# Talking-heads attention and two MLPs: engines a step apart, whole-array scores, values in runs, other operand offsets

## The chip, the cores and the metric

The kernel runs on one core of a Trainium2 chip. The metric is the device time of one execution in microseconds, the median of a few runs. The engines are TensorE (PE; PEld is its weight load), VectorE (DVE), ScalarE (ACT), GpSimd (POOL) and the queue of SyncE (SP), which issues all DMAs.

## What is computed

Four batches of 12 heads, 448 positions, head size 64; then two MLPs on the 1792 x 768 result.

```python
scores = scale * np.matmul(q, k.transpose(0, 1, 3, 2))
scores = np.einsum('bhij,hg->bgij', scores, w_pre)
scores = scores - np.max(scores, axis=-1, keepdims=True)
attn = np.exp(scores)
attn = attn / (np.sum(attn, axis=-1, keepdims=True) + 1e-09)
attn = np.einsum('bhij,hg->bgij', attn, w_post)
x = np.matmul(attn, v)            # then x as rows of 768
h = x @ w_in                      # MLP 1: where(h > 0, h, exp(min(h, 0)) - 1) @ w_out
h = x @ w_in                      # MLP 2: square(max(h, 0)) @ w_out
```

## The kernel before

Precise products are made of fp32r parts: a number is split into a high part (a rounding copy, `hi`) and the rest (`lo`), and three matmuls, hi with hi, hi with lo and lo with hi, add up in one PSUM bank. mix_post and values use plain fp32, for which the trace has two records a matmul.

**Attention** goes through 16 chunks, four a batch, of 120 or 110 queries (`CHUNKS`, L20). `scores` (L156) makes one pair of heads: the keys and queries of the even head lie on partitions 0 to 63, those of the odd one on 64 to 127, so that two 64-row matmuls work side by side, three passes a pair; ScalarE copies both results to `sc`. For each group of ten queries there is a step `t`, 180 in all: `gather` (L174) fetches the group's rows of all heads by DMA, `split` (L180) makes its parts (ScalarE `gh`, GpSimd `gl`), `mix_pre` (L188) mixes the heads in three matmuls, takes the maximum (VectorE) and the exponential with its sum (ScalarE), `weigh` (L201) folds the sum into the weights of the second mix (VectorE), and `mix_post` (L210) mixes again, four matmuls, which VectorE copies to `at`. `values` (L226) multiplies two heads of a chunk by v, in two halves of the array's columns side by side, 8 matmuls (16 records) a call, six calls a chunk; after three calls VectorE copies the result to `xs`.

The order is written out by hand (L319 ff.): step t gathers for t + 8, mixes for t + 2, weighs for t + 1, then makes the scores that are due (one pair in every second step), splits for t + 5, does the other extras (a values call in every second step, loads, splits of keys and queries) and then mix_post of t. Each engine and the DMA queue of SP take their instructions in that order. PSUM has eight banks: three for scores ("qk"), two for "mix", two for "post", one for "pv" (`BANKS`, L45).

**MLPs** (`Mlps.run`, L540): two halves of 896 rows; in each half four layers, of 576, 576, 576 and 672 matmuls. The first three move 448 columns of activations over 128 x 128 of weights; the last one moves 384 columns of weights. `Weights` loads, converts and splits the weights a few units ahead. The first byte of the moving and of the stationary operand in a line of 256 bytes is set by `MOVING` and `STATIONARY` (L25, L26), by half and layer: in the first half 128 and 224 everywhere; in the second half moving 192, 64, 128, 192 and stationary 224, 224, 96, 224. `plan` (L482) puts the first weights and the first MLP's inputs into the last steps of attention.

Of the kernel before, what the change touches and what calls it, by code (L numbers as in the profile page):

```python
# [24 lines left out]
MOVING = (128, 128, 128, 128), (192, 64, 128, 192)  # L25
STATIONARY = (224, 224, 224, 224), (224, 224, 96, 224)  # L26
# [5 lines left out]
def talking_heads_two_mlps(ctx: ExitStack, tc: tile.TileContext, qr, kr, vr, w_pre, w_post, diagonal,  # L32
# [8 lines left out]
    attention(tc, psum, qr, kr, vr, w_pre, w_post, diagonal, xd, mlps)  # L41
# [3 lines left out]
BANKS = {"qk": 3, "mix": 2, "post": 2, "pv": 1}  # L45
# [6 lines left out]
def attention(tc, psum, qr, kr, vr, w_pre, w_post, diagonal, xd, mlps):  # L52
    nc = tc.nc
    with ExitStack() as ctx:
# [6 lines left out]
        AHEAD, SPLIT, PRE = 8, 5, 2  # L61
# [7 lines left out]
        rows = work.tile([120, NR], F32, name="rows")  # L69

# [36 lines left out]
        kh, kl, kraw, qs, qraw = {}, {}, {}, {}, {}  # L107

        def load_k(b, j, raw=None, pairs=((0, 2),)):

            raw = early.tile([128, 2, S], F32, name="kraw", bufs=2) if raw is None else raw
            src = kr[b, :, 4 * j * S : (4 * j + 4) * S].rearrange("d (p a j) -> d a p j", p=2, a=2)
            for x, y in pairs:
                for a in range(2):
                    nc.sync.dma_start(out=raw[64 * a : 64 * a + 64, x:y], in_=src[:, a, x:y])
            kraw[b, j] = raw

        def split_k(b, p, hi_copy=nc.scalar.copy, engine=nc.gpsimd):

            j, a = divmod(p, 2)  # L120
            if a == 0:
                kh[b, j] = early.tile([128, 2, S], F32R, name="kh", bufs=4)
                kl[b, j] = early.tile([128, 2, S], F32R, name="kl", bufs=4)
            raw, hi, lo = (x[b, j][:, a, :] for x in (kraw, kh, kl))
            hi_copy(hi, raw)
            engine.tensor_tensor(lo, raw, hi.bitcast(F32), ALU.subtract)

        def load_q(n, i, raw=None):

            b, c = chunks[n]  # L130
            raw = early.tile([128, 3, CH + 1], F32, name="qraw", bufs=2)[:, :, :CH] if raw is None else raw
            at = (c * H + 6 * i) * CH
            src = qr[b, :, at : at + 6 * CH].rearrange("d (p a i) -> d a p i", p=3, a=2)
# [4 lines left out]
        def split_q(n, i, engine=nc.gpsimd):  # L138
            if i == 0:
                qs[n] = [early.tile([128, H // 2, CH], F32R, name=f"qs{a}", tag=f"qs{a}", bufs=2) for a in "hl"]  # L140
            raw, (hi, lo) = qraw.pop((n, i)), (x[:, 3 * i : 3 * i + 3, :] for x in qs[n])
            nc.vector.tensor_copy(hi, raw)
            engine.tensor_tensor(lo, raw, hi.bitcast(F32), ALU.subtract)

# [9 lines left out]
        sc = {}  # L154

        def scores(n, p, tags=("qk", "qk"), copies=(nc.scalar.copy, nc.scalar.copy)):  # L156

            b, c = chunks[n]
            if p == 0:
                sc[n] = score[(n + 1) % 2].tile([CH, H, S], F32, name="sc", bufs=1)  # L160
            out = [bank(psum, tag)[:CH, :S] for tag in tags]
            h, l = 0, 1
            for k, (x, y) in enumerate(((h, h), (h, l), (l, h))):
                for a in range(2):
                    o = slice(64 * a, 64 * a + 64)
                    nc.tensor.matmul(out[a], qs[n][x][o, p, :], (kh, kl)[y][b, p // 2][o, p % 2, :],  # L166
                                     start=(k == 0), stop=(k == 2))
            for a in range(2):
                copies[a](sc[n][:, 2 * p + a, :], out[a])  # L169


        graw, parts, ex, wg, at, xs, pv = {}, {}, {}, {}, {}, {}, {}
# [7 lines left out]
        def split(t, engine=nc.gpsimd):  # L180
            x = graw.pop(t)
            hi = work.tile([120, S], F32R, name="gh", bufs=SPLIT - PRE + 1)
            lo = work.tile([120, S], F32R, name="gl", bufs=SPLIT - PRE + 1)
# [4 lines left out]
        def mix_pre(t):  # L188
# [5 lines left out]
            nmax = work.tile([120, 1], F32, name="nmax", bufs=PRE + 2)  # L194
            nc.vector.tensor_reduce(nmax, p, AX.X, ALU.max, negate=True)  # L195
            e = work.tile([120, S], F32, name="ex", bufs=PRE + 1)
            tot = work.tile([120, 1], F32, name="tot", bufs=PRE + 2)
            nc.scalar.activation(e, p, AF.Exp, bias=nmax, scale=1.0, accum_out=tot)  # L198
            ex[t] = e, tot

        def weigh(t):  # L201
            e, tot = ex[t]
            nc.vector.tensor_scalar_add(tot, tot, 1e-9)  # L203
            rec = work.tile([120, 1], F32, name="rec", bufs=4)
            nc.vector.reciprocal(rec, tot)
            w = work.tile([120, 120], F32, name="wg", bufs=3)
            nc.vector.tensor_scalar_mul(w.rearrange("p (a k) -> p a k", a=3), post[:, :, :40], rec)  # L207
            wg[t] = w

        def mix_post(t):  # L210
# [3 lines left out]
            e, _ = ex.pop(t)  # L214
# [4 lines left out]
            o, p = at[n][:, :, :, g * NR : (g + 1) * NR], p.rearrange("p c (g r) -> p c g r", r=NR)  # L219
            if t < last:  # L220
                nc.vector.tensor_copy(o, p)  # L221
            else:
                nc.vector.tensor_copy(o[:, :3], p[:, :3])
                nc.scalar.copy(o[:, 3], p[:, 3])

        def values(n, i):  # L226
# [3 lines left out]
            if c == 0 and i == 0:  # L230
                xs[b] = work.tile([128, KC, S], F32, name="xs", bufs=1)
# [90 lines left out]
        for t in range(T):  # L322
# [4 lines left out]
            if t + 1 < T:  # L327
                weigh(t + 1)
# [342 lines left out]
```

## Time and profile before

| | |
|---|---|
| median of 3 runs | 1405.91 us (1405.33 to 1406.09) |
| the profiled execution | 1404.66 us |
| its span | 1402.9 us |
| mean granted TensorE clock | 0.996 |
| TensorE busy | 1388.5 us (99%), 8908 matmul records |
| its weight loads | 1241.3 us (88%) |
| VectorE, ScalarE, GpSimd busy | 876.6, 678.2, 260.7 us |
| DMA | 174.41 MB, queue q1 38.4% of 16 engines |
| first mix_post, first MLP matmul | at 25.73 us, at 465.36 us |

The span is the time from the first to the last instruction of the profiled execution; the rest of its time lies around it. Busy times of engines overlap. A busy TensorE need not be at its peak: matmuls are pipelined, and the time from one start to the next says what one costs.

### The profile page before, as it was taken

What the parts mean: (1) busy time and instruction counts of PE and PEld (TensorE: products, weight loads), DVE (VectorE), ACT (ScalarE), POOL (GpSimd) and SP (SyncE); (2) the same over time, 40 slices, a digit from 0 to 9 for tenths busy, and PEclk for the clock granted to TensorE, in tenths of its full rate; (3) what the DMA queues carried; (4) which work ended last, traced back from release to release, by engine and by line L of the source; (5) the groups of instructions that cost most, each with busy time, mean ns of one, the idle gap of its engine ahead of it and who ended that gap; (6) DMA issues with size and microseconds to landing.
All of it is one profiled execution on the core that took longest, in us unless ns stands there. A gap on an engine that the chain in (4) does not pass through costs nothing.

```text
span 1402.9 us, 24375 instructions
## 1 busy us (share of the span) xinstructions
PE 1388.5 (99%) x8908; PEld 1241.3 (88%) x8908; DVE 876.6 (62%) x2020; ACT 678.2 (48%) x1507; POOL 260.7 (19%) x241
## 2 busy tenths in 40 slices
PE   8999999999999999999999999999999999999998
PEld 5777778787777899999999999999999999999998
DVE  6877777777788699866699997634441123443121
ACT  5776676676667576533255543235551113333111
POOL 2575565475557000000000000000000000000000
PEclk8999999999999999999999999999999999999999
DMA  4633542543625455554455576531221111112131
GB/s 144 182 112 109 182 131 103 176 140 107 193 99 168 164 175 169 192 173 159 136 162 169 167 239 207 166 113 52 57 75 46 60 45 46 51 51 63 40 107 40
DMA packets 104907, 174.41 MB, mean 124 GB/s; under 512 B 22771, under 2 KB 82259, under 8 KB 104787
## 3 DMA queue, kind: packets, MB, share of 16 engines
q1 hardware_dynamic: 104787, 172.85, 38.4%
q8 instruction: 70, 1.15, 0.3%
q14 instruction: 50, 0.41, 0.1%
HBM read 97.93 MB, written 36.18 MB: 96 GB/s over the span
## 4 chain that ended last, share of the span: by engine, by line
PE 97%; DVE 1%; DMA 0%; SPq 0%; issue 0%; ACT 0%; POOL 0%; DVEq 0%; POOLq 0%
PE ps_post L218 12%; PE ps_qk L537 8%; PE ps_qk L538 8%; PE ps_qk L536 8%; PE ps_pv L237 6%; PE ps_mix L536 6%; PE ps_post L537 6%; PE ps_mix L537 6%; PE ps_mix L538 6%; PE ps_post L538 6%; PE ps_post L536 6%; PE ps_qk L166 5%; PE ps_pv L537 3%; PE ps_pv L538 3%; PE ps_pv L536 3%; PE ps_mix L193 3%
## 5 line engine op out<-in xcount | busy, mean ns | idle before, releaser
L423 ACT CAST wh<-wf 128x384 fp32r<-128x384 f32 (+1 forms) x240 | 126.7, 532 | 271.5 <-DVE wf L409 112.2
L424 DVE TENSOR_TENSOR wl<-wf,wh 128x384 fp32r<-128x384 f32 (+1 forms) x240 | 140.4, 588 | 159.2 <-ACT wh L423 154.5
L185 POOL TENSOR_TENSOR gl<-graw,gh 120x448 fp32r<-120x448 f32 x178 | 203.0, 1141 | 194.7 <-ACT gh L184 167.9
L218 PE MATMUL ps_post<-wg,ex 120*112 120x120 f32 x1440 | 189.4, 275 | 3.0 <-DVE wg L207 2.9
L218 PEld LDWEIGHTS ps_post<-wg,ex 120*112 120x112 f32 x1440 | 165.3, 178 | 29.7 <-issue 10.7
L198 ACT ACTIVATE ex<-ps_mix,nmax 120x448 f32<-120x448 f32 x180 | 114.3, 635 | 129.0 <-DVE tot L203 123.9
L221 DVE COPY at<-ps_post 112x480 f32<-112x480 f32 x161 | 105.4, 655 | 68.6 <-PE ps_post L218 67.5
L195 DVE TENSOR_REDUCE nmax<-ps_mix 120x1 f32<-120x448 f32 x180 | 111.8, 621 | 2.8 <-PE ps_mix L193 2.2
L537 PE MATMUL ps_qk<-xl,wh 128*128 128x448 f32 x288 | 105.3, 365 | 0.0
L538 PE MATMUL ps_qk<-xh,wl 128*128 128x448 f32 x288 | 105.2, 365 | 0.0
L536 PE MATMUL ps_qk<-xh,wh 128*128 128x448 f32 x288 | 104.9, 364 | 0.0
L184 ACT CAST gh<-graw 120x448 fp32r<-120x448 f32 x180 | 102.4, 571 | 0.4 <-DMA graw<-sc 0.4
L237 PEld LDWEIGHTS ps_pv<-at,v 112*64 112x64 f32 x1536 | 74.1, 136 | 29.4 <-issue 20.6
L237 PE MATMUL ps_pv<-at,v 112*64 112x110 f32 (+2 forms) x1536 | 93.9, 265 | 1.3 <-DVE xs L242 0.7
L169 ACT COPY sc<-ps_qk 120x448 f32<-120x448 f32 x176 | 84.6, 534 | 7.1 <-PE ps_qk L166 6.4
L558 DVE TENSOR_TENSOR tmp<-tmp 128x448 f32<-128x448 f32 x64 | 39.9, 624 | 73.7 <-ACT tmp L557 73.7
L191 PE MATMUL ps_mix<-gh,pre_l 120*120 120x448 f32 x180 | 80.0, 444 | 3.0 <-ACT gh L184 3.0
L385 ACT ACTIVATE wf<-wd 128x384 f32<-128x384 f32 (+1 forms) x120 | 69.3, 577 | 16.0 <-DMA wd<-w1i 10.8
L562 DVE TENSOR_TENSOR hl<-tmp,hh 128x448 fp32r<-128x448 f32 x128 | 74.2, 619 | 0.4
L409 DVE SCALAR_TENSOR_TENSOR wf<-wd,wf 128x384 int32<-128x384 int32 (+1 forms) x120 | 70.3, 586 | 4.1
L407 DVE SCALAR_TENSOR_TENSOR wf<-wd,wf 128x384 int32<-128x384 int32 (+1 forms) x120 | 70.2, 585 | 4.1
L537 PE MATMUL ps_mix<-xl,wh 128*128 128x448 f32 x192 | 70.2, 365 | 0.0
(166 smaller groups left out, 3298.4 us busy)
## 6 DMA issues: line engine op xcount, KB each, us to landing
graw<-sc SPq DMA_DIRECT2D x180, 210.0 KB
wd<-w1i SPq DMA_DIRECT2D x32, 384.0 KB
wd<-w1o SPq DMA_DIRECT2D x24, 512.0 KB
wd<-w2i SPq DMA_DIRECT2D x32, 384.0 KB
wd<-w2o SPq DMA_DIRECT2D x32, 384.0 KB
w1if<-wf SPq DMA_DIRECT2D x32, 192.0 KB
w1of<-wf SPq DMA_DIRECT2D x24, 256.0 KB
w2if<-wf SPq DMA_DIRECT2D x32, 192.0 KB
```

What stands on the lines that cost most here:

```text
L184: nc.scalar.copy(hi, x)
L185: engine.tensor_tensor(lo, x, hi.bitcast(F32), ALU.subtract)
L195: nc.vector.tensor_reduce(nmax, p, AX.X, ALU.max, negate=True)
L198: nc.scalar.activation(e, p, AF.Exp, bias=nmax, scale=1.0, accum_out=tot)
L218: nc.tensor.matmul(p[:, c, :], e[:, c * NJ : (c + 1) * NJ], w, start=True, stop=True)
L221: nc.vector.tensor_copy(o, p)
L237: nc.tensor.matmul(pv[n][o : o + 64, i % 3, :w], vt[b, i // 3][:, jc, g % 6 * D : (g % 6 + 1) * D], at[n][:, jc, g, :w], start=(jc == 0), ...
L423: nc.scalar.copy(hi, f)
L424: nc.vector.tensor_tensor(lo, f, hi.bitcast(F32), ALU.subtract)
L536: mm(p, wh, xh, start=first, stop=False)
L537: mm(p, wh, xl, start=False, stop=False)
L538: mm(p, wl, xh, start=False, stop=last)
```

## The change

- **Order in a step.** Groups are gathered nine steps ahead, split six, mixed four; the maximum and exponential (`maxima`) become a function of their own, three ahead. Copies out of PSUM stand a step behind the matmuls that filled the bank: `keep_scores`, `keep_weighed` and `keep_x` empty lists that `scores`, `mix_post` and `values` filled in the step before. `weigh` does two steps at once. The banks are 2 "qk", 3 "mix", 2 "post", 1 "pv".
- **Scores on the whole array** (all chunks but the first four): each query and key is loaded twice, so that partition 2d + a holds entry d. `split_k` subtracts `odd` times the rounded key, with `odd` 0 or 1 by partition, which leaves the high part on even partitions and the low part on odd ones in one tile `kp`. A head then is two matmuls, the queries' hi and lo against `kp`, and is put into a step alone (or two, where twelve heads don't fit nine or ten steps). `odd` is made by two memsets, a DMA to DRAM and one back. The casts of these keys and queries are ScalarE's, the subtractions GpSimd's.
- **Values.** The six calls of a chunk stand in two runs of three, in steps 1 and 2 of the next chunk, behind mix_post. Each run's result goes to DRAM on its own, four steps later, instead of once a batch.
- **MLPs.** `MOVING, STATIONARY = 128, 224` for both halves. The first two units' `part` is split over two steps (`part_hi`, `part_lo`), and the bank order ends in "mix" instead of "qk".

The order on TensorE in an early chunk of attention, before (L191 to L193 are mix_pre, L166 scores, L237 values, L218 mix_post):

```order
L191 MATMUL ps_mix<-gh,pre_l 120x448
L192 MATMUL ps_mix<-gh,pre_h 120x448
L193 MATMUL ps_mix<-gl,pre_h 120x448
L166 MATMUL ps_qk<-kh,qsh 120x448 x2
L166 MATMUL ps_qk<-kl,qsh 120x448 x2
L166 MATMUL ps_qk<-kh,qsl 120x448 x2
L237 MATMUL ps_pv<-at,v 64x110 x8
L218 MATMUL ps_post<-wg,ex 112x120 x4
L191 MATMUL ps_mix<-gh,pre_l 120x448
L192 MATMUL ps_mix<-gh,pre_h 120x448
L193 MATMUL ps_mix<-gl,pre_h 120x448
L218 MATMUL ps_post<-wg,ex 112x120 x4
```

And now (L252 to L254 are mix_pre, L228 and L229 one head's scores, L288 mix_post, L314 values):

```order
L252 MATMUL ps_mix<-gh,pre_l 120x448
L253 MATMUL ps_mix<-gh,pre_h 120x448
L254 MATMUL ps_mix<-gl,pre_h 120x448
L228 MATMUL ps_qk<-kp,qp 120x448
L229 MATMUL ps_qk<-kp,qp 120x448
L288 MATMUL ps_post<-wg,ex 112x120 x4
L252 MATMUL ps_mix<-gh,pre_l 120x448
L253 MATMUL ps_mix<-gh,pre_h 120x448
L254 MATMUL ps_mix<-gl,pre_h 120x448
L288 MATMUL ps_post<-wg,ex 112x120 x4
L314 MATMUL ps_pv<-at,v 64x110 x24
```

Steps with a pair of scores and a values call have become steps with one head, and steps with three values calls in a row.

SP's queue at the start, before (L73, L74 load the mixing weights, L135 the queries of chunk 1, L177 is the gather):

```order
L73 DMA both<-w_pre 120x1x12
L73 DMA both<-w_post 120x1x12
L74 DMA rows<-diagonal 120x10
L135 DMA q_room<-qr 64x3x120 x4
L177 DMA graw<-sc 120x1x448 x9
```

And now (L78, L79 are the two DMAs of `odd`):

```order
L83 DMA both<-w_pre 120x1x12
L83 DMA both<-w_post 120x1x12
L84 DMA rows<-diagonal 120x10
L78 DMA turns_d<-turns 1x128
L79 DMA odd<-turns_d 128x1
L146 DMA q_room<-qr 64x3x120 x4
L238 DMA graw<-sc 120x1x448 x10
```

The queries of chunk 1 stand behind a DMA that waits for another one's landing.

VectorE's queue near the end of attention, around the first subtraction of a weight's parts, before (L223 copies mix_post's result, L195 is the maximum, L203 to L207 `weigh`, L424 the subtraction):

```order
L207 TENSOR_SCALAR wg<-post,rec 120x120
L424 TENSOR_TENSOR wl<-wf_5914,wh 128x384
L223 COPY at<-ps_post 112x36x10
L195 TENSOR_REDUCE nmax<-ps_mix 120x1
L203 TENSOR_SCALAR tot<-tot 120x1
```

And now (L296, L260, L272 to L277 and L532 in the same roles):

```order
L277 TENSOR_SCALAR wg<-post,rec 120x120 x2
L532 TENSOR_TENSOR wl<-wf_5792,wh 128x384
L260 TENSOR_REDUCE nmax<-ps_mix 120x1
L296 COPY at<-ps_post 112x36x10 x2
L272 TENSOR_SCALAR tot<-tot 120x2
```

The subtraction still stands ahead of a maximum, one step behind the cast it reads.

The diff, cut to its core:

```diff
-MOVING = (128, 128, 128, 128), (192, 64, 128, 192)
-STATIONARY = (224, 224, 224, 224), (224, 224, 96, 224)
+MOVING, STATIONARY = 128, 224
-BANKS = {"qk": 3, "mix": 2, "post": 2, "pv": 1}
+BANKS = {"qk": 2, "mix": 3, "post": 2, "pv": 1}
-        AHEAD, SPLIT, PRE = 8, 5, 2
+        AHEAD, SPLIT, MIX, MAX, QN, LATE = 9, 6, 4, 3, 3, 4
+        WIDE = len(CHUNKS)
+        def load_odd():
+            for a in range(2):
+                nc.gpsimd.memset(turns[:, :, a : a + 1], float(a))
+            nc.sync.dma_start(out=turns_d, in_=turns.rearrange("o d a -> o (d a)"))
+            nc.sync.dma_start(out=odd, in_=turns_d.rearrange("o p -> p o"))
+        def twice(out, src):
+            nc.sync.dma_start(out=out, in_=src.unsqueeze(1).broadcast_to([D, 2, src.shape[1]]))
+        def split_k(b, h):
...
+            hi = early.tile([128, S], F32R, name="khi", bufs=1)
+            nc.scalar.activation(hi, raw, AF.Copy, scale=odd)
+            nc.gpsimd.tensor_tensor(k, raw, hi.bitcast(F32), ALU.subtract)
+        def scores(n, h):
...
+            hi, lo = (x[:, h % QN, :] for x in qp[n, h // QN])
+            k = kp[b, h // 2][:, h % 2, :]
+            nc.tensor.matmul(out, hi, k, start=True, stop=False)
+            nc.tensor.matmul(out, lo, k, start=False, stop=True)
+            taken.append((sc[n][:, h, :], out))
+            when = [start + h * steps // H for h in range(H)]
+            for h in range(H):
+                put(when[h], scores, n, h)
+            for i in range(H // QN):
+                put(when[QN * i] - 6, load_q, n, i)
+                put(when[QN * i] - 3, split_q, n, i)
+        for b in range(1, B):
+            for h in range(H):
+                t = first[WIDE * b - 1] - AHEAD + 4 - (H - 1 - h) * 12 // 5
+                put(max(0, t - 4), load_k, b, h)
+                put(t, split_k, b, h)
-                put(first[n + 1] + (2 + i if n == N - 1 else min(2 * i + 1, 10 if n == N - 2 else 11)), values, n, i)
+                put(first[n + 1] + (2 if n == N - 1 else 1) + i // 3, values, n, i)
-                put(first[n] + 9, load_v, b, 1)
+                put(first[n] + 4, load_v, b, 1)
+        for t in range(T + 3):
+            beside = extra.pop(t, ())
+            if t + AHEAD < T:
+                gather(t + AHEAD)
+            keep_scores()
+            if t + SPLIT < T:
+                split(t + SPLIT)
+            if t + MAX < T:
+                maxima(t + MAX)
+            if t + MIX < T:
+                mix_pre(t + MIX)
+            for f, a in beside:
+                if f in (scores, first_scores):
+                    f(*a)
+            store_x(t)
+            keep_weighed()
+            keep_x(t)
+            if t < T:
+                mix_post(t)
+            for f, a in beside:
+                if f is values:
+                    f(*a)
+            weigh(t + 1)
...
```

## Rows read from the trace of the kernel before

**Rows 1.** Page, part 4, the chain that ended last by engine.

```profile
PE 97%; DVE 1%; DMA 0%; SPq 0%; issue 0%; ACT 0%; POOL 0%; DVEq 0%; POOLq 0%
```

**Rows 2.** Timeline of TensorE, attention: start us, us, engine line op, tiles, count.

```profile
301.24 0.44 PE L191 MATMUL ps_mix<-gh,pre_l 120*120 120x448 f32 x1
...
302.81 0.97 PE L237 MATMUL ps_pv<-at,v 112*64 112x110 f32 x16
...
304.55 0.44 PE L191 MATMUL ps_mix<-gh,pre_l 120*120 120x448 f32 x1
...
306.95 0.44 PE L191 MATMUL ps_mix<-gh,pre_l 120*120 120x448 f32 x1
...
309.48 0.45 PE L191 MATMUL ps_mix<-gh,pre_l 120*120 120x448 f32 x1
309.76 0.36 PE L192 MATMUL ps_mix<-gh,pre_h 120*120 120x448 f32 x1
309.96 0.37 PE L193 MATMUL ps_mix<-gl,pre_h 120*120 120x448 f32 x1
...
310.91 0.44 PE L191 MATMUL ps_mix<-gh,pre_l 120*120 120x448 f32 x1
```

**Rows 3.** Timeline of TensorE, end of attention (in brackets: idle before, and releaser).

```profile
454.37 1.05 PE L218 MATMUL ps_post<-wg,ex 120*112 120x120 f32 x8 [2.43 <-DVE wg L207]
...
459.86 2.44 PE L237 MATMUL ps_pv<-at,v 112*64 112x108 f32 x48 [0.63 <-DVE at L223]
462.99 2.44 PE L237 MATMUL ps_pv<-at,v 112*64 112x108 f32 x48 [0.69 <-DVE xs L242]
```

**Rows 4.** Timeline of TensorE, first matmuls of six of the MLPs' eight layers.

```profile
580.68 0.36 PE L536 MATMUL ps_mix<-hh,wh 128*128 128x448 f32 x1
...
695.88 0.36 PE L536 MATMUL ps_mix<-xh,wh 128*128 128x448 f32 x1
...
927.55 0.37 PE L536 MATMUL ps_pv<-xh,wh 128*128 128x448 f32 x1
...
1045.31 0.37 PE L536 MATMUL ps_pv<-hh,wh 128*128 128x448 f32 x1
...
1163.58 0.36 PE L536 MATMUL ps_qk<-xh,wh 128*128 128x448 f32 x1
...
1282.61 0.34 PE L536 MATMUL ps_qk<-wh,hh 128*128 128x384 f32 x1
```

**Rows 5.** Windows in layers 2, 4, 7, 8: PE, PEld, DVE, ACT, POOL, clock, DMA.

```profile
585.00:685.00 100.00, 100.00 (x502) 93.84 (x501) 67.47 (x121) 30.53 (x55) 0.00 (x0) 1.00 0.49 164
...
820.00:920.00 100.00, 100.00 (x579) 100.00 (x578) 71.31 (x152) 33.74 (x68) 0.00 (x0) 1.00 0.60 197
...
1170.00:1270.00 100.00, 100.00 (x485) 90.97 (x484) 44.37 (x82) 38.88 (x83) 0.00 (x0) 1.00 0.18 52
1290.00:1390.00 100.00, 100.00 (x579) 100.00 (x578) 17.14 (x31) 15.13 (x30) 0.00 (x0) 1.00 0.18 56
```

**Rows 6.** Timeline of all engines, the kernel's start.

```profile
10.93 2.65 SPq L135 DMA_DIRECT2D q_room<-qr  x4
...
15.58 0.35 DVE L142 CAST qsh<-q_room 128x360 fp32r<-128x360 f32 x1 [0.52 <-DMA q_room<-qr]
...
24.00 3.32 POOL L185 TENSOR_TENSOR gl<-graw,gh 120x448 fp32r<-120x448 f32 x3 [22.75 <-ACT gh L184]
```

**Rows 7.** Timeline of VectorE, end of attention.

```profile
450.37 2.25 DVE L424 TENSOR_TENSOR wl<-wf,wh 128x384 fp32r<-128x384 f32 x1 [1.09 <-ACT wh L423]
```

**Rows 8.** Timeline of ScalarE, two steps of attention.

```profile
301.21 0.59 ACT L184 CAST gh<-graw 120x448 fp32r<-120x448 f32 x1
301.68 0.58 ACT L125 CAST kh<-kraw 128x448 fp32r<-128x448 f32 x1
302.85 0.64 ACT L198 ACTIVATE ex<-ps_mix,nmax 120x448 f32<-120x448 f32 x1 [0.58 <-DVE tot L203]
...
303.47 0.96 ACT L169 COPY sc<-ps_qk 120x448 f32<-120x448 f32 x2
```

More of the change, by code (lines that the diff above doesn't have):

```diff
@@ L103, in width @@
             return min(ng * NR, S - at * NR)
[L107 to L112, printed above, removed]
+        k_room = work.tile([128, 3, 2, S], F32, name="k_room", tag="at", bufs=2)
+        q_room = work.tile([128, 2, H // 2, CH], F32, name="q_room", tag="v", bufs=3)
@@ L116, in load_k, with split_first_k @@
-            kraw[b, j] = raw
-        def split_k(b, p, hi_copy=nc.scalar.copy, engine=nc.gpsimd):
+                    nc.sync.dma_start(out=k_room[64 * a : 64 * a + 64, j, x:y], in_=src[:, a, x:y])
+        def split_first_k(p):
             j, a = divmod(p, 2)
             if a == 0:
[L122 to L133, printed above, removed]
+                k0[j] = [key_tile() for _ in "hl"]
+            raw, (hi, lo) = k_room[:, j, a, :], (x[:, a, :] for x in k0[j])
+            nc.vector.tensor_copy(hi, raw)
+            nc.vector.tensor_tensor(lo, raw, hi.bitcast(F32), ALU.subtract)
@@ L151, in load_v, with score_tile, first_scores @@
             nc.sync.dma_start(out=vt[b, i], in_=src[:, :, i * DM // 2 : (i + 1) * DM // 2])
-        sc = {}
-        def scores(n, p, tags=("qk", "qk"), copies=(nc.scalar.copy, nc.scalar.copy)):
-            b, c = chunks[n]
+        sc, taken, weighed, summed, stored = {}, [], [], [], []
+        def score_tile(n):
+            sc[n] = score[(n + 1) % 2].tile([CH, H, S], F32, name="sc", bufs=1)
+        def first_scores(n, p, tags=("qk", "qk"), copies=(nc.scalar.copy, nc.scalar.copy), now=False):
             if p == 0:
-                sc[n] = score[(n + 1) % 2].tile([CH, H, S], F32, name="sc", bufs=1)
+                score_tile(n)
             out = [bank(psum, tag)[:CH, :S] for tag in tags]
@@ L165, in scores @@
                     o = slice(64 * a, 64 * a + 64)
-                    nc.tensor.matmul(out[a], qs[n][x][o, p, :], (kh, kl)[y][b, p // 2][o, p % 2, :],
+                    nc.tensor.matmul(out[a], q0[n, p // 3][x][o, p % 3, :], k0[p // 2][y][o, p % 2, :],
                                      start=(k == 0), stop=(k == 2))
-            for a in range(2):
-                copies[a](sc[n][:, 2 * p + a, :], out[a])
-        graw, parts, ex, wg, at, xs, pv = {}, {}, {}, {}, {}, {}, {}
+            if now:
+                for a in range(2):
+                    copies[a](sc[n][:, 2 * p + a, :], out[a])
+            else:
+                taken.extend((sc[n][:, 2 * p + a, :], out[a]) for a in range(2))
+        def scores(n, h):
+            b, c = chunks[n]
+            if h == 0:
+                score_tile(n)
+            out = bank(psum, "qk")[:CH, :S]
+            hi, lo = (x[:, h % QN, :] for x in qp[n, h // QN])
[3 more added lines that the diff above has]
+            taken.append((sc[n][:, h, :], out))
+        graw, parts, mixed, ex, tot, wg, at, pv = {}, {}, {}, {}, {}, {}, {}, {}
         def gather(t):
@@ L241, in values, with keep_x, store_x @@
             if i % 3 == 2:
-                nc.vector.tensor_copy(xs[b][:, i - 2 : i + 1, r0 : r0 + w], pv[n][:, :, :w])
-            if i % 3 == 2 and c == len(CHUNKS) - 1:
-                nc.sync.dma_start(out=xd[b][:, i - 2 : i + 1, :], in_=xs[b][:, i - 2 : i + 1, :])
+                summed.append((xd[b][:, i - 2 : i + 1, r0 : r0 + w], pv[n][:, :, :w]))
+        def keep_x(t):
+            for o, p in summed:
+                x = work.tile([128, 3, CH], F32, name="xs", bufs=3)[:, :, : o.shape[2]]
+                nc.vector.tensor_copy(x, p)
+                stored.append((t + LATE, o, x))
+            summed.clear()
+        def store_x(t):
+            while stored and stored[0][0] <= t:
+                _, o, x = stored.pop(0)
+                nc.sync.dma_start(out=o, in_=x)
         extra = {}
@@ L503, in plan @@
         for i in range(2 * KC):
[L504 removed]
+            put(last + 2 + i, self.load_x, i)
             put(last + 6 + i, self.split_x, i)
```

213 lines of the change are left out of this document (124 added, 89 removed).

## The prediction

> **What bounds the kernel.** The page says it at once: TensorE carries 97% of the chain that ended last, ScalarE and GpSimd none of it [rows 1]. So every term below is TensorE time, or time in which it would have to wait. The second view is TensorE's timeline of four steps in the middle of attention [rows 2]. A step runs from one first mix_pre matmul (L191) to the next, and there are four kinds: with scores and values 3.31 us (301.24 to 304.55), with scores 2.40, with values 2.53, with neither 1.43. Scores thus cost 0.97 alone, values 1.10 alone, both together 1.88. In a bare step matmuls of 448 columns on the whole array follow at 0.20 (309.76 to 309.96): three are 0.60, and mix_post takes the other 0.83. A score call is three passes of two 64-row matmuls side by side; at 0.20 a pass it would be 0.60, and it costs 0.97. So 0.37 goes into leaving the whole-array shape and coming back. The same for values, which work in two halves of 64 columns: a run of three calls shows 2.44, one call 0.97, so a further call costs (2.44 - 0.97) / 2 = 0.735 [rows 2, 3], and of a lone call's 1.10 some 0.365 is the change of shape.
>
> The third view is where the layers of the MLPs begin [rows 4]. From 580.68 to 695.88 the second layer of the first half takes 115.20 for its 576 matmuls, 200.0 ns each. The same layers of the second half take 117.76, 118.27 and 119.03 (927.55, 1045.31, 1163.58, 1282.61), with the same work, at the same granted clock of 1.00 (2.4 GHz), and beside less DMA (share 0.18 against 0.49 [rows 5]). What the code has different there is the operands' offsets.
>
> **MLP offsets.** With 128 and 224 everywhere, the second half is the first half again: -(2.56 + 3.07 + 3.83) = **-9.5 us**. The last layer also changes its moving offset, 192 to 128; the two last layers show 579 matmuls in 100 us each [rows 5], so that is 0.
>
> The Trainium skill (SBUF — State Buffer, section Who interferes with whom) holds that inside the engine side only the port pair of VectorE and GpSimd causes contention, and its section Operand start alignment asks no more of a start than a multiple of the element size. By that, offsets of TensorE's operands are worth nothing, and this term would be 0; the layers above disagree, by up to 3.3%.
>
> **TensorE in the attention loop.** The 180 mix_pre and mix_post calls stay, so I count what is added to bare steps. Before, in the order: 30 steps with scores, 34 with values, 54 with both, and two value calls between the last mix_post: 30 x 0.97 + 34 x 1.10 + 54 x 1.88 + 2 x 1.10 = 170.2. After: 144 heads of two whole-array matmuls, no change of shape next to mix_pre, 144 x 0.40 = 57.6; chunks 2 and 3 keep the pairs, 12 x 0.97 = 11.6; 30 runs of three values calls, 30 x (1.10 + 2 x 0.735) = 77.1. Sum 146.3, **-23.9 us**. The heads themselves are dearer (four passes for a pair's three, +14.4); 84 changes of shape (2 x 12 + 2 x 30) in place of 294 (2 x 30 + 2 x 34 + 3 x 54 + 2 x 2) pay for it.
>
> The operands of scores and mix_pre also land at other offsets: 540 + 288 matmuls at 200 ns [rows 2] up to the worst layer's 119.03 / 576 = 206.6 [rows 4] is 0 to 5.5. I take +1, as mix_pre shows 200 now at offsets that are not 128 and 224 either.
>
> **Start.** SP gets two DMAs in its queue ahead of chunk 1's queries, the second of which reads what the first wrote. Queries issued at 10.93 for 2.65 land by 15.58 [rows 6], so a landing takes some 2 us: the queries come about 2.4 later, and with them half of chunk 1's scores, whose copies stand ahead of the first gh cast on ScalarE. Then the first mix_post stands behind mix_pre of steps 2 to 4, not 2: two more GpSimd subtractions, 3.32 / 3 = 1.1 each [rows 6], +2.2, less two mix_pre of 0.60 that are then done. **+3.4**; between +1 (the landing hidden by chunk 0's scores) and +7 (twice the 3.4, if the delayed queue and the deeper start add up with nothing beside them).
>
> **End.** Before, mix_post waits 2.43 for its weights and the last values 0.63 and 0.69 [rows 3]; the 2.43 is VectorE's wl subtraction of 2.25, for which the next maximum stood in line [rows 7]. The second values run gets a bank of its own: -0.7. The subtraction is now a step behind its cast, but stays in VectorE's queue beside GpSimd's x splits, so I leave the 2.43. **-0.7**, between -3.1 (it goes) and +1.5 (steps without scores last 1.43 now, so VectorE has less time beside them to catch up; two thirds of the 2.25 once more).
>
> **The other engines.** ScalarE is next. From start to start: gh cast 0.47, exponential with its read 0.62, two copies at most 0.96 [rows 8]. In the nine score steps of a chunk of eleven that makes 9 x 1.09 and, at 0.47, 12 copies, 4 query casts and (one in 2.4 steps) 3.75 key casts, 19.1, against TensorE's 9 x 1.43 + 12 x 0.40 = 17.7; the two values steps then give 8.0 against 2.2. So ScalarE falls behind by 1.4 where keys are cast, and recovers. Each result is used a step later than before (copies lead ScalarE's next step, and mix_post and mix_pre, 1.4, pass on TensorE meanwhile), which covers it. GpSimd has one subtraction for each cast, (9 + 4 + 3.75) x 1.1 = 18.4 at most, and works two steps ahead: covered. VectorE loses 90 additions and reciprocals and the later query casts. On SP the halves of v now load a step apart; the gathers behind them are issued nine steps ahead. For what leaks through **+1**, between 0 and 17 (that 1.4 lost in each of 12 phases).
>
> **Sum.** -9.5 - 23.9 + 1 + 3.4 - 0.7 + 1 = -28.7 on the profiled run's 1404.66 (span 1402.9 and 1.76 around it): 1376.0. The median of the runs is 1.25 above that run, so **1377**.
>
> **Rivals.**
> *Offsets are not the cause* of the slow half (something that comes with the second half is): 1377 + 9.5 = 1386.5. Against it: each layer there has its own pace [rows 4], and the last layer none [rows 5]. 3%. By the rule of the Trainium skill above (SBUF — State Buffer) it would be so.
>
> *ScalarE becomes the bound*: score phases run at its pace, and the upper end of that term comes in full, 17 for 1: 1377 + 16 = 1393. For it: the 19.1 against 17.7. Against: the chain has no ScalarE in it today [rows 1]. 8%.
>
> *Heads lose as pairs did* (slower): the 0.37 belongs not to the shape but to every score call, as a wait for its bank (only two are left for scores) or its first weights. Then a head costs 0.77: 144 x 0.37 = 53 more, 1430. It turns the result once a head loses over 28.7 / 144 = 0.20. Against: mix_pre also opens a bank per call and loses nothing behind mix_post, and scores with values lose 0.545 together rather than 0.735, as if sharing a change [rows 2]. 4%.
>
> *Packing is worth its passes*: what is lost around scores and values stays with those steps whatever the shape, and the heads' extra passes come on top: -9.5 + 14.4 + 4.7 = +9.6, 1415. The same rows speak against it. 2%. The Trainium skill (TensorEngine Tiling (Array Packing), When to Use Tiling) recommends two-row packing for a contraction of 64, for up to twice the rate, and so speaks against undoing it; its Key Properties also say that a change of mode drains the engine, which the 0.37 bears out.
>
> **Numbers.** The forecast has 83%. Its own ends: all good, -9.5 - 23.9 + 1 - 3.1 = -35.5, 1370; all bad, start +6, offsets +4, end 0, waits +8, -15.4, 1390. Range 1370 to 1390, which holds the first rival too and leaves out the others. Faster by over 0.2% (about what a measurement of this kernel tells from none): forecast and first two rivals, 0.94; slower 0.05; within 0.2% 0.01, where the losing rivals come halfway.
>
> **What would show it.** The three layers at 115.2 each; steps of 1.43, 1.83 (one head), 2.23 (two) and about 4.0 (values) on TensorE; score matmuls at 0.20 with no gap behind mix_pre; first mix_post near 29 to 31; no TensorE wait on ScalarE or GpSimd over a few us in all. The forecast is wrong if whole-array scores pay a loss per head, if waits for ex, sc or gl fill the score phases, or if the second half of the MLPs keeps its 118 us.

## The result and the profile after

The changed kernel takes **1389.17 us** (median of nine runs), against 1405.33 in the same series: a ratio of 0.9895 (95% interval 0.9868 to 0.9922). The direction was right, but the gain is 16 us instead of 29, just over half of it. The profiled run took 1388.04, its span 1386.0, against 1404.66 and 1402.9. The forecast for that run was 1376.0, so 12 us are missing. Single executions of most kernels here take some 11 us more; the profiles of e6_spread and e9_together are two of these, with 119.1, 119.0 and 119.0 in the first three MLP layers where the others have 115.3, 115.2 and 115.2, for a cause that stays open, so those two profiles are compared over attention alone.

The chain that ended last, its shares by engine, is the first view again:

```profile
PE 93%; DVE 2%; DMA 2%; ACT 1%; SPq 1%; POOL 1%; issue 1%; POOLq 0%; DVEq 0%; ACTq 0%
```

Before, TensorE had 97% [rows 1]. It is still the bound, but 7% of the chain now belongs to others, where 3% did: TensorE waits more.

What TensorE does itself came out as forecast. Its timeline in the middle of attention (start, duration, engine, line, operation, out<-in, count):

```profile
304.93 0.47 PE L252 MATMUL ps_mix<-gh,pre_l 120*120 120x448 f32 x1
...
306.55 2.48 PE L314 MATMUL ps_pv<-at,v 112*64 112x110 f32 x48
308.96 0.47 PE L252 MATMUL ps_mix<-gh,pre_l 120*120 120x448 f32 x1
...
309.68 0.37 PE L228 MATMUL ps_qk<-kp,qp 128*120 128x448 f32 x1
309.88 0.37 PE L229 MATMUL ps_qk<-kp,qp 128*120 128x448 f32 x1
310.09 0.36 PE L228 MATMUL ps_qk<-kp,qp 128*120 128x448 f32 x1
...
311.24 0.45 PE L252 MATMUL ps_mix<-gh,pre_l 120*120 120x448 f32 x1
...
313.09 0.44 PE L252 MATMUL ps_mix<-gh,pre_l 120*120 120x448 f32 x1
```

From one first mix_pre to the next: a step with values 4.03 (304.93 to 308.96), with two heads 2.28, with one head 1.85. The score matmuls (309.68, 309.88, 310.09) follow mix_pre and each other at 0.20, with no gap. Forecast were 4.0, 2.23 and 1.83; medians over the kernel are 4.04, 2.25 and 1.84.

The same timeline where the layers of the MLPs' second half begin:

```profile
920.25 0.36 PE L644 MATMUL ps_pv<-xh,wh 128*128 128x448 f32 x1
...
1035.45 0.36 PE L644 MATMUL ps_pv<-hh,wh 128*128 128x448 f32 x1
...
1150.65 0.36 PE L644 MATMUL ps_mix<-xh,wh 128*128 128x448 f32 x1
...
1265.85 0.34 PE L644 MATMUL ps_mix<-wh,hh 128*128 128x384 f32 x1
```

Three layers of 115.20 stand where 117.76, 118.27 and 119.03 stood [rows 4]. That term was forecast to a tenth.

So the missing 12 us are waits. TensorE's list of them (line, what it waited for, us in total, times, longest):

```profile
PE ps_mix L252 <- ACT gh L245: 3.8, 3, 1.7
PE ps_qk L228 <- ACT sc L302: 1.9, 2, 1.4
PE ps_post L288 <- DVE wg L277: 1.6, 2, 1.4
PE ps_post L212 <- DVE qp L158: 1.6, 1, 1.6
PE ps_post L288 <- ACT at L297: 1.4, 2, 0.9
```

These totals are small, because the list has only gaps of over 0.15 us. Slower steps show more: what the steps from 60 us on take beyond the median of their kind (same matmuls between two first mix_pre) adds up to 8.9 us in the changed kernel and to 1.1 in the kernel before. By place: the first mix_post comes at 31.45 (25.73 before), and from there to the first MLP matmul it takes 426.6 (439.6 before), 13.0 less. The forecast's terms for that part made 23.8 less (-23.9 + 1 + 1 - 0.7, and the 1.2 of mix_pre done ahead of it).

What holds TensorE is seen one engine further back. The timeline near the end of attention, where mix_post waits longest for its weights (in brackets: idle before, and what ended it):

```profile
441.57 1.15 POOL L246 TENSOR_TENSOR gl<-graw,gh 120x448 fp32r<-120x448 f32 x1
441.60 2.24 DVE L272 TENSOR_SCALAR tot<-tot 120x2 f32<-120x2 f32 x1
...
442.67 1.15 POOL L639 TENSOR_TENSOR xl<-tmp,xh 128x448 fp32r<-128x448 f32 x1
...
443.88 0.17 DVE L274 RECIPROCAL rec<-tot 120x2 f32<-120x2 f32 x1
444.08 0.58 DVE L277 TENSOR_SCALAR wg<-post,rec 120x120 f32<-120x120 f32 x2
444.56 1.04 PE L288 MATMUL ps_post<-wg,ex 120*112 120x120 f32 x8 [1.40 <-DVE wg L277]
...
445.22 0.63 ACT L264 ACTIVATE ex<-ps_mix,nmax 120x448 f32<-120x448 f32 x1 [2.79 <-DVE nmax L260]
```

An addition of two numbers per partition takes 2.24 us. It starts just after GpSimd's subtraction and ends at 443.84, where GpSimd's second subtraction ends too (442.67 + 1.15 = 443.82). Weights, maxima and exponentials queue behind it. All additions of that line, in the kernel before (first) and in the changed one (count, duration in ns as minimum/median/maximum):

```profile
L203 DVE TENSOR_SCALAR tot<-tot x180: 139/145/153, 23.5 to 456.2; 120x1 f32<-120x1 f32 x180
```

```profile
L272 DVE TENSOR_SCALAR tot<-tot x90: 152/472/2241, 28.4 to 449.6; 120x2 f32<-120x2 f32 x90
```

With one column none of 180 took over 0.153, though 144 of them met a running subtraction on GpSimd, that is, started while one had 0.15 us or more to go. With two columns 60 of 90 met one, and 58 of these end within 0.06 us of the end of a subtraction.

### The profile page after: what moved, and what is told of

Same layout as the page of the kernel before. It is cut to its first block, busy times and chain, and to the rows that moved or that the text cites. A ratio compares the mean times of both kernels' runs of the same rounds, so it can differ in the third digit from the quotient of the medians.

```text
span 1386.0 us, 23859 instructions
## 1 busy us (share of the span) xinstructions
PE 1366.1 (99%) x8764; PEld 1270.2 (92%) x8764; DVE 865.1 (62%) x1812; ACT 703.8 (51%) x1578; POOL 304.1 (22%) x285
## 3 DMA queue, kind: packets, MB, share of 16 engines
q8 instruction: 69, 1.13, 0.3%
## 4 chain that ended last, share of the span: by engine, by line
PE 93%; DVE 2%; DMA 2%; ACT 1%; SPq 1%; POOL 1%; issue 1%; POOLq 0%; DVEq 0%; ACTq 0%
PE ps_post L288 9%; PE ps_mix L644 8%; PE ps_mix L646 8%; PE ps_mix L645 8%; PE ps_qk L646 6%; PE ps_post L646 6%; PE ps_post L644 6%; PE ps_qk L644 6%; PE ps_qk L645 6%; PE ps_post L645 6%; PE ps_pv L314 5%; PE ps_pv L646 3%; PE ps_pv L645 3%; PE ps_pv L644 3%; PE ps_mix L252 3%; PE ps_mix L254 2%
## 5 line engine op out<-in xcount | busy, mean ns | idle before, releaser
L532 DVE TENSOR_TENSOR wl<-wf,wh 128x384 fp32r<-128x384 f32 (+1 forms) x240 | 138.7, 581 | 157.2 <-ACT wh L525 153.3
L288 PEld LDWEIGHTS ps_post<-wg,ex 120*112 120x112 f32 x1440 | 173.5, 178 | 18.2 <-issue 4.7
L288 PE MATMUL ps_post<-wg,ex 120*112 120x120 f32 x1440 | 180.4, 268 | 3.3 <-DVE wg L277 1.6
L264 ACT ACTIVATE ex<-ps_mix,nmax 120x448 f32<-120x448 f32 x180 | 117.6, 653 | 42.0 <-DVE nmax L260 41.9
L245 ACT CAST gh<-graw 120x448 fp32r<-120x448 f32 x180 | 105.7, 590 | 27.7 <-POOL gl L246 9.3
L260 DVE TENSOR_REDUCE nmax<-ps_mix 120x1 f32<-120x448 f32 x180 | 111.0, 617 | 8.5 <-PE ps_mix L254 8.5
L644 PE MATMUL ps_mix<-xh,wh 128*128 128x448 f32 x288 | 104.5, 363 | 0.0
L645 PE MATMUL ps_mix<-xl,wh 128*128 128x448 f32 x288 | 104.4, 362 | 0.0
L646 PE MATMUL ps_mix<-xh,wl 128*128 128x448 f32 x288 | 104.4, 362 | 0.0
L252 PE MATMUL ps_mix<-gh,pre_l 120*120 120x448 f32 x180 | 81.5, 453 | 4.6 <-ACT gh L245 3.8
L314 PE MATMUL ps_pv<-at,v 112*64 112x110 f32 (+2 forms) x1488 | 78.2, 262 | 0.6 <-DVE at L296 0.6
L314 PEld LDWEIGHTS ps_pv<-at,v 112*64 112x64 f32 x1488 | 71.6, 137 | 4.4 <-DVE at L296 0.8
L644 PE MATMUL ps_post<-xh,wh 128*128 128x448 f32 x192 | 69.6, 362 | 0.0
```

The source lines that it names most:

```text
L245: nc.scalar.copy(hi, x)
L252: nc.tensor.matmul(p, pre_l, hi, start=True, stop=False)
L288: nc.tensor.matmul(p[:, c, :], e[:, c * NJ : (c + 1) * NJ], w, start=True, stop=True)
L314: nc.tensor.matmul(pv[n][o : o + 64, i % 3, :w], vt[b, i // 3][:, jc, g % 6 * D : (g % 6 + 1) * D], at[n][:, jc, g, :w], start=(jc == 0), ...
L532: self.nc.vector.tensor_tensor(lo, self.single.pop(i), hi.bitcast(F32), ALU.subtract)
L644: mm(p, wh, xh, start=first, stop=False)
```

## The experiments

Thirteen kernels ran. Those that aren't the kernel before with an edit are the changed kernel with the edit shown.

**The offsets alone** (e1_offsets, on the kernel before).

```
-MOVING = (128, 128, 128, 128), (192, 64, 128, 192)
-STATIONARY = (224, 224, 224, 224), (224, 224, 96, 224)
+MOVING = (128,) * 4, (128,) * 4
+STATIONARY = (224,) * 4, (224,) * 4
```

> The kernel before with one edit: operand offsets 128 and 224 in both halves of the MLPs. If offsets cause the slow half, layers 5 to 7 take 115.2 each in place of 117.76, 118.27 and 119.03, attention is unchanged, and the time is 1405.3 - 9.5 = 1396 (ratio 0.9933). If something else in the change made those layers fast (less DMA from attention's end, another order of banks), they keep their 118 and the ratio is 1.000.

Measured: 1396.43, ratio 0.9945 (0.993 to 0.996). The three layers take 115.2 each; attention keeps its 1.43, 2.42, 2.51 and 3.33 per kind of step. The offsets are the cause, and the term is right. The profiled run gains 8.2 and not 9.5, as its granted clock falls to 0.50 (1.2 GHz) once more, from 455.4 to 458.8 us, and two values calls, a mix_post and two more values calls take 4.4 there in place of 2.8.

**The addition one column at a time** (e2_add).

```
-            nc.vector.tensor_scalar_add(both, both, 1e-9)
+            for i in range(2):
+                nc.vector.tensor_scalar_add(both[:, i : i + 1], both[:, i : i + 1], 1e-9)
```

> The changed kernel with the addition of 1e-9 done on one column at a time (180 instructions of 120x1, as in the kernel before, in place of 90 of 120x2). Theory A: an addition of two columns stands until GpSimd's running subtraction ends (76 of the 90 met one; mean 0.57 in place of 0.16, up to 2.24), which makes maxima and weights late, and TensorE's waits behind them. Then the additions take 0.15 each, the wait of 1.40 for wg at 444.6 and the 1.36 for a score bank at 405.8 go, and the time falls by 3 to 5 us (some 1385). Theory B: the additions stand beside TensorE's work, and what is missing lies elsewhere (start, gathers): durations fall, the time stays within 1 us of 1389.

Measured: 1379.83, ratio 0.983 (0.9814 to 0.9847), 9.3 less than the changed kernel: theory A, and twice what it made of it. All additions of e2_add in the same view:

```profile
L273 DVE TENSOR_SCALAR tot<-tot x180: 136/144/154, 27.7 to 440.3; 120x1 f32<-120x1 f32 x180
```

129 of these 180 meet GpSimd, and none is held. The first MLP matmul moves from 458.03 to 448.79; 0.6 of these 9.2 us are an earlier first mix_post, which the edit doesn't touch, and 8.6 come behind it. What steps from 60 us on take beyond their kind's median falls from 8.9 to 2.2; both waits named in the expectation are gone. Twice as many additions, and a faster kernel.

**Why this addition, and not the multiplication for wg** (e14_post40, with e2_add's edit). The reciprocal of 120x2 and the multiplication of 120x120 meet GpSimd as often (64 of 90 and 125 of 180 in e2_add) and are not held; the multiplication reads its tile in three rows of 40 out of 41 columns, and writes 120 in one row.

```
-        post = work.tile([120, 3, 41], F32, name="post")
+        post = work.tile([120, 3, 40], F32, name="post")
```

> The changed kernel with additions of one column, and the tile post with rows of 40 columns in place of 41, so that the 120x120 multiplications for wg read it without a gap. Theory A: VectorE is held where a single-source operation from SBUF to SBUF covers an even, gapless extent (the addition of 120x2 was, the one of 120x1 and the multiplication out of the 41-column tile were not, 125 of which met GpSimd and took 0.336 each); then the 180 multiplications, 0.336 now, are held to the end of GpSimd's subtraction when they meet one, with a mean of 0.6 to 0.9, and the time rises from e2_add's 1379.8 by 5 to 25. Theory B: something particular to the addition in place on two columns (its own output read by the next instruction, the merge of two steps) caused the holding: multiplications stay at 0.34 and the time within 1 of 1379.8.

Measured: 1392.54, ratio 0.9904 (0.9872 to 0.9937), 12.7 more than e2_add. The multiplication in e2_add (first) and here:

```profile
L278 DVE TENSOR_SCALAR wg<-post,rec x180: 326/334/341, 28.2 to 441.0; 120x120 f32<-120x120 f32 x180
```

```profile
L278 DVE TENSOR_SCALAR wg<-post,rec x180: 269/603/1319, 29.7 to 455.9; 120x120 f32<-120x120 f32 x180
```

Left alone it is faster now (0.277 for 0.336), and when it meets GpSimd (109 times) it takes 0.99 in the median. So theory A: not the merging of two steps, but the shape of the operands decides; whether it is the gap or the odd number of rows is not separated. The operation counts too, for the reciprocal of e2_add, of the same 120x2 that held the addition, is never held:

```profile
L275 DVE RECIPROCAL rec<-tot x90: 165/166/167, 28.0 to 440.5; 120x2 f32<-120x2 f32 x90
```

The Trainium skill (VectorE: DVE Perf Modes, Mode 2×_2P — use both read ports for one tensor) says of instructions like tensor_scalar that with a single source, from SBUF to SBUF, with outermost extents that are even (or odd and equal in source and destination), they stream the two halves through two ports. The Trainium skill (SBUF — State Buffer, Who interferes with whom) adds that the second pair of ports is shared with GpSimd under an exclusive lock. These runs agree: additions of 120x1 and multiplications from 3 rows into 120 stay free, those of 120x2 and of 120 into 120 are held, 0.14 against up to 2.24 us for the additions.

**Values spread as before** (e6_spread, with e2_add's edit).

```
-                put(first[n + 1] + (2 if n == N - 1 else 1) + i // 3, values, n, i)
+                put(first[n + 1] + (2 + i // 3 if n == N - 1 else min(2 * i + 1, 10)), values, n, i)
```

> The changed kernel with additions of one column (as in the run e2_add, 1379.8) and the six values calls of a chunk one in every second step, as in the kernel before, in place of two runs of three. It tests the term of the forecast that each change of shape on TensorE costs 0.365. Theory A: 90 lone calls in place of 30 runs are 60 more changes, 60 x 0.365 = +21.9, 1401.7; a step with one head and one lone values call takes 1.84 + 1.10 = 2.94. Theory B: the price belongs to the calls (their operands, their bank) and not to the shape: the time stays at 1380, within 3.

Measured: 1406.4, ratio 0.9992 (0.9961 to 1.0023); from first mix_post to first MLP matmul 436.4 against e2_add's 418.0, +18.4. A lone call adds 1.06 (steps of 1.86 become 2.92), a run of three 2.59, so splitting a run costs 3 x 1.06 - 2.59 = 0.59, and 30 runs 17.7. So theory A in kind: the price belongs to going into a run and out of it, not to the call. It is 0.29 each, not the forecast's 0.365. That the change of shape is what costs it, and not something else at a run's ends, fits whole-array scores that pay nothing, but no run here has values in another shape.

**Copies in the same step** (e9_together, with e2_add's edit).

```
-            keep_scores()
             if t + SPLIT < T:
...
+            keep_scores()
             store_x(t)
-            keep_weighed()
             keep_x(t)
             if t < T:
                 mix_post(t)
+            keep_weighed()
```

> The changed kernel with additions of one column, and with copies of scores and of at issued in the same step as the matmuls that they read, as in the kernel before, in place of the next step. Theory A: with TensorE's steps at 1.43 to 2.25 the delay of one step is needed, since VectorE and ScalarE otherwise stand in order behind results of the running step: TensorE waits in most score steps, at least 0.1 in each of 108, +10 or more. Theory B: mix_pre four steps and gathers nine steps ahead cover it: within 3 of 1379.8.

Measured: 1443.04, ratio 1.0252 (1.0201 to 1.0303); first mix_post to first MLP matmul 476.4, +58 on e2_add: theory A. Steps with one head take 2.58 in the median, not 1.84. TensorE's largest wait there:

```profile
PE ps_post L289 <- DVE wg L278: 31.2, 52, 1.4
```

VectorE's copy of at waits for the end of the running mix_post, and the next weights stand behind it. The order one step apart is what makes the short steps possible; without it the other edits would have lost to the kernel before.

**The start and the gathers.** Five kernels, all but e3_v and e5_pro with e2_add's edit. e3_v loads v's second half at step 9, as before; e7_odd issues load_odd behind the first gathers; e5_pro puts casts first while the pipeline fills; e8_start has these two, and both halves of the first v behind the fifth gather; e10_add_pro is e5_pro and e2_add alone. The edits of e3_v, e7_odd, e8_start and e5_pro:

```
-                put(first[n] + 4, load_v, b, 1)
+                put(first[n] + 9, load_v, b, 1)
```

```
-        load_odd()
         first_q(1, 0)
...
             gather(t)
+        load_odd()
```

```
             gather(t)
+            if t == 4:
+                load_v(0, 0)
+                load_v(0, 1)
...
-            if c == 0:
+            if c == 0 and b:
                 put(first[n] + 3, load_v, b, 0)
```

```
         for t in range(MIX):
+            split(t + 2)
             mix_pre(t)
             if t < MAX:
                 maxima(t)
-            split(t + 2)
```

> The changed kernel with the second half of v loaded nine steps into a batch, as in the kernel before, in place of four. Theory A: between 38 and 53 us the DMA engines are the bound (busy share 0.96 from 40 to 50), and 672 KB of v ahead of the gathers make ScalarE's gh casts wait 2.9 for graw; then the steps at 47 to 57 lose 2 of their 3.3 us of excess, and the time falls by 1.5 to 2. Theory B: the doubled key loads alone keep the DMA engines full there, and the time stays within 0.7 of 1389.

> The changed kernel with additions of one column and the two DMAs of odd issued behind the first nine gathers in place of ahead of chunk 1's queries. Theory A, the forecast's: the queries come 2.4 earlier; TensorE's wait of 1.6 for them at 17 goes, and first mix_post and the whole come 1.5 to 2 earlier than in e2_add (1379.8), 1378. Theory B: copies of chunk 0's scores and the first gathers set the first mix_pre anyway; first mix_post within 0.5 of 30.8, time unchanged.

> The changed kernel with the gh and gl of step t+2 issued ahead of the maxima and exponential of step t while the pipeline is filled. Theory A: the start is long (first mix_post 31.45 against 25.73) because ScalarE does gh 2 to 5 behind exponentials that wait for maxima; then gh 2 starts at about 23.2 in place of 25.2, the first mix_post comes at about 27.5 to 28.5, and the time falls by 3 to 4 (some 1385.5). Theory B, as forecast: two more GpSimd subtractions of 1.1 set it, in a chain that the order on ScalarE does not change: first mix_post within 1 us of 31.4, the time unchanged.

> The changed kernel with four edits: additions of one column, odd behind the gathers, casts ahead of exponentials while the pipeline fills, and both halves of v of the first batch issued behind the fifth gather (about 24 us, where the DMA share was 0.3) in place of steps 3 and 4. Theory A: the losses add up: e2_add 1379.8, less 2 (odd), less 3.0 (the filling took 5.69 in place of 8.66 in e5_pro), less 2 (the late gathers at 47 to 57), 1373. Theory B: the DMA engines are full from 38 to 53 by the keys alone, or the v ahead of gathers delays the first steps: nothing for that edit, 1375 or more.

> The changed kernel with additions of one column and with casts ahead of exponentials while the pipeline fills; nothing else. Theory A: the order on ScalarE is what made the start long, and its gain (from first mix_pre to first mix_post 8.7 in the changed kernel and e2_add, 5.7 in e5_pro) stays: 3.0 less than e2_add's 1379.8, 1376.8. Theory B: from 36 to 57 us the DMA engines set the pace (busy share 0.7 to 1.07), so what is gained ahead of them is waited for there, as in e7_odd, where an earlier queue only moved the waits: 1379 to 1380, with the twelfth mix_post at 58 as in e2_add.

Measured: e3_v 1388.14 (0.9881, 0.9868 to 0.9894), e7_odd 1380.26 (0.9804, 0.9766 to 0.9842), e5_pro 1387.39 (0.9892, 0.9865 to 0.9918), e8_start 1378.19 (0.979, 0.9756 to 0.9823), e10_add_pro 1381.16 (0.9842, 0.9817 to 0.9867). With the casts ahead, first mix_pre to first mix_post takes 5.7 in place of 8.7 (e5_pro, e8_start, e10_add_pro) and 4.8 before, so the two more subtractions of the forecast weren't the main price: the order on ScalarE was. Part of the 3.0 is TensorE's clock. The windows of 24 to 32 us in the changed kernel (first) and in e5_pro (from:to, length, busy time and count of PE, PEld, DVE, ACT, POOL, granted clock, DMA share, GB/s):

```profile
24.00:28.00 4.00, 2.56 (x8) 1.44 (x6) 1.35 (x3) 2.26 (x6) 2.14 (x2) 0.69 0.29 110
28.00:32.00 4.00, 3.08 (x9) 1.76 (x8) 2.11 (x7) 3.19 (x8) 2.36 (x4) 0.50 0.28 108
```

```profile
24.00:28.00 4.00, 2.99 (x12) 1.49 (x10) 3.31 (x7) 3.06 (x9) 2.41 (x3) 1.00 0.38 136
28.00:32.00 4.00, 3.76 (x25) 3.22 (x26) 3.40 (x10) 3.14 (x9) 4.00 (x4) 1.00 0.47 163
```

In the changed kernel TensorE, busy for 2.31 of the 4 us from 20, falls to the lower level (1.2 GHz) at 25.5, and its own matmuls, 0.38 from start to start in place of 0.20, then lengthen the chain; in e5_pro it has 2.4 GHz in both windows. The kernel before fell too, from 22.6 to 29.4 us. How the 3.0 divide between order and clock is not separated.

Where the additions are split, little of it arrives. The mix_post of step 12 comes at 58.2 in e2_add, 60.0 in e7_odd, 58.9 in e10_add_pro and 59.5 in e8_start: there an earlier load or step only moves the wait. e7_odd lost 1.5 in one step at 46.7, e8_start 3.8 in one at 26.4. In e5_pro more of it stays: step 12 comes at 56.9 against 59.9 in the changed kernel, the first MLP matmul 2.4 earlier. So theory B for the time of e7_odd, e8_start and e10_add_pro, and in e3_v by its trace (first MLP matmul at 457.83 against 458.03; 1.0 in the medians is not a difference that these runs resolve); e5_pro lies between its two.

What the delay by load_odd is worth at the first mix_post stays open, between 0.1 and 1.6 us. Without it chunk 1's queries are cast at 14.3 (e7_odd) and not at 16.0 (e2_add). The first mix_post is at 30.78 and 30.84 in these two; but in e6_spread and e9_together, which ran beside e7_odd and have e2_add's start, it is at 32.4, 1.6 later. TensorE was at 1.2 GHz while it made some of chunk 1's scores in those two and in e7_odd, but not in e2_add, which makes the larger figure the likelier one.

**Fewer bytes in that stretch** (e11_keys: e10_add_pro and)

```
-                t = first[WIDE * b - 1] - AHEAD + 4 - (H - 1 - h) * 12 // 5
+                t = first[WIDE * b - 1] - AHEAD + 4 - (H - 1 - h) * (15 if b == 1 else 24) // 10
```

> As e10_add_pro, and the doubled keys of the second batch loaded from step 9 on, one in 1.5 steps, in place of step 0 on, one in 2.4 (the last at the same step). It takes some 1 MB of the 6.2 MB that the DMA engines move from 30 to 60 us out of that stretch. Theory A: these bytes make the gathers late; TensorE's excess of 40 to 60 us (2.2 in e2_add, 4.0 in e7_odd) falls under 1, and the time is 2 less than e10_add_pro's. Theory B: the gathers are late for their own queue or the v loads alone: the excess and the time stay within 0.7.

Measured: 1375.18, ratio 0.9809 (0.978 to 0.9837), 6 less than e10_add_pro (4.9 by the place of the first MLP matmul): theory A, and more than it said. TensorE's excess of 40 to 60 us is 4.6 in e10_add_pro and 0.4 here. The windows from 40 to 56 us in e10_add_pro (first) and in e11_keys:

```profile
40.00:44.00 4.00, 4.00 (x31) 3.12 (x29) 2.29 (x7) 3.47 (x9) 3.98 (x4) 1.00 1.02 237
44.00:48.00 4.00, 2.42 (x18) 1.59 (x16) 2.25 (x5) 2.05 (x5) 1.43 (x2) 1.00 0.90 211
48.00:52.00 4.00, 3.64 (x26) 2.86 (x26) 1.13 (x5) 1.70 (x5) 1.06 (x1) 1.00 0.76 211
52.00:56.00 4.00, 3.43 (x20) 2.10 (x18) 3.18 (x10) 4.00 (x12) 3.77 (x5) 1.00 0.66 178
```

```profile
40.00:44.00 4.00, 4.00 (x31) 3.25 (x31) 3.46 (x11) 3.40 (x9) 3.19 (x4) 1.00 0.99 237
44.00:48.00 4.00, 4.00 (x32) 3.25 (x31) 2.49 (x7) 2.40 (x7) 1.21 (x2) 1.00 0.77 218
48.00:52.00 4.00, 4.00 (x30) 2.97 (x30) 3.30 (x10) 4.00 (x11) 2.42 (x4) 1.00 0.84 225
52.00:56.00 4.00, 4.00 (x34) 3.54 (x31) 3.42 (x10) 4.00 (x12) 3.12 (x4) 1.00 0.76 238
```

With keys and v together the DMA share is 1.02 and 0.90 for 8 us; TensorE is then busy for only 2.42 of the 4 us from 44, and VectorE, ScalarE and GpSimd for 1.13, 1.70 and 1.06 of the 4 us from 48, for want of gathered rows. ScalarE's waits for these from 36 to 58 us are 4.8 in e10_add_pro; in the changed kernel and in e11_keys:

```profile
ACT gh L245 <- DMA graw<-sc: 3.7, 2, 2.9
```

```profile
ACT gh L245 <- DMA graw<-sc: 1.6, 1, 1.6
```

The mix_post of step 12 comes at 53.8, where e10_add_pro has 58.9. The edit takes the casts and subtractions of the same keys out of these steps too; that the bytes counted more is read from the waits for rows, and no run separates the two.

**Without the addition, and all together** (e12_noadd is e5_pro's edit and the first line here; e13_all is both lines and e11_keys' edit).

```
-            nc.vector.tensor_scalar_add(both, both, 1e-9)
...
-                put(first[n] + 4, load_v, b, 1)
+                put(first[n] + 6, load_v, b, 1)
```

> As e10_add_pro, without the additions of 1e-9 (left out of the computation; they stand beside sums of at least 1). VectorE loses 180 instructions, 26 us. Theory A: only the holding of VectorE counted, not its busy time, which TensorE's steps cover: within 0.7 of e10_add_pro. Theory B: VectorE's time itself is near the bound in the score steps: 2 or more below e10_add_pro.

> The edits of e11_keys and e12_noadd together, and the second half of each v loaded at step 6 in place of 4. If DMA bytes bound the steps of 36 to 57 us, spreading both v and keys takes their whole excess: 3 below e10_add_pro, 1374. If not, it equals e11_keys within 0.7.

Measured: e12_noadd 1378.94 (0.9811, 0.9799 to 0.9824), e13_all 1373.53 (0.9769, 0.9756 to 0.9781). Without the addition the kernel is 2 below e10_add_pro, but its profile shows the difference in the stretch of 40 to 60 us, where runs differ anyway, so whether VectorE's time itself counts stays open. e13_all is 1.7 below e11_keys, not a difference that these runs resolve (0.3 by the first MLP matmul, 444.00 against 444.33): what the later half of v adds to the later keys doesn't show. It beats both kernels: 32 us less than before, 15.6 less than the changed one. Its chain gives TensorE 97%, as the kernel before.

## Why the prediction was half right

**MLP offsets**: -9.5 forecast, -9.5 in the trace, -8.4 by e1_offsets' median. Right, and the rival against it is out. The rule that the prediction drew from the Trainium skill (SBUF — State Buffer, Operand start alignment) goes beyond that section, which says of itself that it is about legality and not speed. Offsets are not all that sets the pace: with 128 and 224 and a granted clock of 1.00 e6_spread has layers of 119.0 in the first half and of 115.2 in the second.

**TensorE in the attention loop**: -23.9 forecast. Score matmuls stand at 0.20 and the median steps of every kind came out within 0.04 of the forecast. In e11_keys, where most waits are gone, first mix_post to first MLP matmul takes 414.7, 25.0 less than before; the forecast's terms for that part made 23.8. Right, with one part mis-sized: a change of shape is 0.29, not 0.365, which a lone call and a run of three measured apart show. The rivals in which heads lose or packing is worth its passes are out, 0.398 being what a head adds.

**The other engines**: this is the step that failed. The prediction put it as "VectorE loses 90 additions and reciprocals", a relief, and gave +1 for all leaks. The merged additions have two columns, and an instruction on 240 numbers became one that waits out a GpSimd subtraction: 8.6 us of TensorE's time by the profile of e2_add, 9.3 by its median. The count of instructions and their busy time were read, not the change in their shape. The row was there: the wl subtraction of 2.25 [rows 7], whose 238 undisturbed instances take 0.55 in the median, stood beside two GpSimd subtractions (449.98 to 452.20): VectorE held, as it now reads. It was priced as a wait at one place; what else on VectorE could be held after the change was not asked. The rivals whose times lie nearest were not the cause: the offsets did work, and with VectorE free ScalarE as the bound has no more than the 2.2 beyond medians.

**Start**: +3.4 forecast, to a first mix_post 4.6 later; it came 5.7 later. The size was nearly right, in part by luck: the queries do come 1.7 later through load_odd, of which 0.1 to 1.6 is left at the first mix_post; the deeper pipeline costs 0.9 with casts ahead (5.7 against 4.8 from first mix_pre to first mix_post), near the 1.0 that the forecast gave it, and 3.0 more through casts that stand behind exponentials on ScalarE, which the forecast did not have. Missed was what follows. That "the halves of v now load a step apart; the gathers behind them are issued nine steps ahead" counted the distance in steps and not the bytes: 6.2 MB from 30 to 60 us against 5.0 before (5.4 from 24 to 54, as its first mix_post is 5.7 earlier). Moving some of the keys out was worth 5 to 6 us (e11_keys), part of it the casts' gain that had been waited away.

**End**: -0.7 forecast, with the 2.43 kept. The 0.7 came. In place of the 2.43 stands the 1.40 for wg, and that came from the addition; it is gone in e2_add.

Together: e2_add's profiled run took 1378.76, 9.3 of the 12.0 less, 8.6 of them behind the first mix_post and so the addition's. The 2.8 that are left to the forecast lie ahead of 60 us, in the start and the late gathers.

## What to carry to other kernels

Merging small instructions is only a saving if the merged shape runs in the same way: look at whether an addition or multiplication on VectorE, with one source between SBUF tiles, gets even, gapless extents, and whether GpSimd is busy beside it. A gap of one column in a tile was worth 12.7 us here and looks like waste. When loads are moved to other steps, add up the bytes of the stretch that they land in; where the DMA share was near 1, reorderings mostly moved the wait, and moving keys out of the stretch is what helped.

## What was not expected of the hardware

A VectorE instruction of 0.16 us stood up to 2.24 us, through two GpSimd subtractions in a row, since the second had started when the first ended. That can go on: in e3_v and e5_pro, which keep this addition, one of them took 4.62 and 4.61 us, through five subtractions, four of which had started after it. The held time is not shown as a wait but as the instruction's own duration, so in the list of waits it appears only as other engines' lateness. And an instruction can be made faster for itself (0.336 to 0.277) and the kernel slower by 12.7 us with it.
